# Turning q and k half by transposes, in a new written order, with stage three's first splits moved

## The chip, the core and the metric

The kernel runs on one core of a Trainium2 chip. Its time is device microseconds of one execution; the kernel before took 529.17 us (median of three runs, 526.91 to 531.14). One more execution was profiled: all durations below are from it.

## What is computed

Three blocks follow each other on four sequences of 576 tokens. The first, for 32 heads of 64 columns (four batches, eight heads), adds a coarse attention over four-token means and a local attention within three tokens to each side:

```python
q_d = q.reshape(B, H, S // 4, 4, D).mean(axis=3)      # k_d, v_d alike
out_d = softmax(q_d @ k_d.T / sqrt(D)) @ v_d
mask = abs(pos[:, None] - pos[None, :]) < 4
out_local = softmax(where(mask, q @ k.T / sqrt(D), -1e9)) @ v
x = repeat(out_d, 4, axis=2) + out_local               # B, S, H * D = 512
```

The second block is a gated MLP (`h = gelu(x @ w_in)`, half of it normed and mixed over tokens by `w_sg`, then `w_out`, plus `x`). The third gives every token the two best of four causal attention experts of 64 columns (`x @ wq[e]`, `wk[e]`, `wv[e]`, softmax, `wo[e]`, weighted by the gate's softmax).

## The kernel before, in words

It has three stages, one after the other: `phase1` (local and coarse attention, up to about 134 us of the span), `phase2` (the MLP, to about 340 us) and `phase3` (the experts).

**Stage one** works on 16 units u, one for each pair of heads of a batch. A unit is a chain of short steps, named by one or two letters and the unit's number. `lq`, `lk`, `lv`, `lw` load q, k, v and the v windows (all on SyncE's queue). `Aq` and `Ak` turn q and k on TensorE (`a_pe`, L325), since the products need the 64 columns of a head on partitions: head 0 goes to partitions 0 to 63 of a PSUM tile, head 1 to 64 to 127. `aq` and `ak` copy that to SBUF on ScalarE, `aqd` and `akd` sum groups of four. `Bd` makes the coarse scores, `Bm` the local mask and `Bs` the local scores; `ym yb ey` and `xm xs ex sx` are the two softmaxes, `ne n ny nx` norm them, `Cc` and `Ca` transpose them back (TensorE), `cb` and `ca` copy, `V` sums v in fours on GpSimd, `Du` and `Do` multiply by v, `du` copies, and `dx` adds both into `xT`, the activations, on VectorE (L520). Between the units stand the steps that split `w_in` into two parts (`fetch size clamp bits stt1 stt2 hi lo`), the first split of x (`xhi`, `xlo`) and four blocks of the first product of stage two (`mul`, `gelu`).

TensorE's matmuls come in three tile shapes. Full tiles (128 by 128) serve `Cc`, `Ca`, `mul` and all of stage two. `Aq`, `Ak` and `Du` use two strips of 64 columns that can work side by side, one for each head: a full-height strip on columns 0 to 63 (strip 0) and one on 64 to 127 (strip 1). `Bm`, `Bd`, `Bs` and `Do` use four quarters of 64 by 64. In float32 a product is two records on TensorE, a transpose one.

The string `ORDER` is the order in which all steps are issued, written out by hand: each engine gets its steps in that order. `Steps.run` walks it. It hands each TensorE step one of three `wide` PSUM tiles or two `narrow` ones: the one that a small cost model (the numbers in `do(...)`) thinks is free first, ties going to the first in the list. Of the three wide tiles `pw` was allocated first (named `wide` in traces and orders), then `wide0` and `wide1` (`wide_134` and `wide_135` in the orders below). `GATE` holds a load back until a named TensorE step. So a load can be late for three reasons: its place in the queue, its gate, or the buffer that it fills.

**Stage two** begins with `turn_next`: it transposes the first part of `w_sg` into the first wide PSUM tile of the stage (`pwsg`), which lies on the banks of `pw`. Then follows the first block of `dv`, and so on.

**Stage three** begins with a short run of products for batch 0 (`run(next(first[k], None) for k in "vvpvpvvpp")`: v is one block of 128 tokens for v and the gate, p one block of q or k), and then walks through (batch, expert, block of rows) steps, where `plan` spreads the work that prepares the next batch over the steps of the one before. Each batch's x is split into a high and a low part first (`jobs_split`: ScalarE copies the high part, VectorE subtracts it). The split x of all batches shares one buffer. PSUM is eight banks, handed out in turn; six handed to nothing (`past0` to `past5`) make the first block of v take the seventh. `cmask` and `tmask`, the causal masks, are made by GpSimd at the start.

Of the kernel before, what the change touches and what calls it, by code (L numbers as in the profile page):

```python
# [8 lines left out]
F32 = mybir.dt.float32  # L9
# [4 lines left out]
ALU = mybir.AluOpType  # L14
# [6 lines left out]
def raw(ap):  # L21
# [9 lines left out]
    Du1 yb4 du1 Cc2 lw1 aqd5 Do0 Bm5 fetch2 ne3 akd6 sx4 cb2 Bd5 dx0 ym5 fetch1 ey4 ne4 Bs5 size0 V2 Ca2 Aq6
    ca2 n3 yb5 aq6 ny3 lw2 V3 lw3 ey5 n4 xm5 Aq7 Ak7 clamp0 ak7 Du2 xs5 aq7 aqd6 bits0 nx3 stt10 Do1 stt20 Bm6
    Bd6 du2 dx1 Cc3 ex5 sx5 cb3 Ca3 ny4 ne5 ym6 hi0 ca3 Bs6 aqd7 lk8 yb6 Cc4 akd7 cb4 Do2 xm6 nx4 n5 Bd7 lq8
    xs6 lv4 Bm7 Ca4 nx5 ey6 dx2 ex6 ca4 ym7 Bs7 Du3 lk9 lo0 sx6 lv5 xm7 lq9 Aq8 ny5 ne6 lq10 Ak8 du3 V4 n6 yb7
    size1 xs7 Do3 clamp1 aq8 ey7 lw4 Ca5 nx6 Du4 lk10 ex7 ak8 ca5 V5 aqd8 du4 Cc5 fetch3 bits1 dx3 stt11 size2
    Ca6 akd8 lq11 Ak9 clamp2 bits2 cb5 stt21 Aq9 stt12 ak9 ny6 Do4 sx7 aq9 ca6 Bd8 aqd9 dx4 Bm8 Cc6 ym8 ne7 Bs8
    yb8 stt22 Ak10 Du5 cb6 xm8 ey8 n7 lv7 hi1 Aq10 ak10 xs8 akd9 Bm9 du5 lo1 akd10 size3 Bd9 clamp3 lv6 ny7
    aq10 Bs9 ym9 nx7 ex8 xm9 aqd10 yb9 lw5 fetch4 lk12 Aq11 Cc7 ey9 bits3 lk11 Bd10 lq12 lw6 xs9 Bm10 aq11
    stt13 V6 Do5 aqd11 ym10 lv8 Bs10 cb7 Ca7 yb10 ey10 stt23 ex9 Du6 dx5 sx8 V7 xm10 hi2 Ak12 du6 ca7 sx9 Du7
    lq13 ne8 Ak11 ak12 Aq12 size4 n8 xs10 ny8 ak11 lo2 aq12 clamp4 Bm11 akd12 nx8 Do6 V8 akd11 ne9 du7 aqd12  # L40
    Cc8 n9 Bd11 lk13 Bs11 dx6 lw7 ym11 bits4 fetch5 ex10 lq14 cb8 Ca8 stt14 xm11 yb11 sx10 Aq13 lk14 ey11 nx9
    lw8 Du8 xs11 ca8 aq13 ny9 Ak13 Do7 hi3 aqd13 ne10 stt24 ex11 dx7 n10 sx11 Bm12 Bd12 ak13 du8 Cc9 size5 Ca9
    ym12 ny10 nx10 lv9 akd13 Bs12 cb9 clamp5 Cc10 xm12 ca9 ne11 Ak14 n11 cb10 yb12 ak14 lo3 bits5 xs12 Aq14 Do8
    Bm13 hi4 ey12 lk15 lq15 ny11 V9 stt15 Bd13 aq14 ex12 dx8 Bs13 Ak15 aqd14 lv10 ym13 Aq15 stt25 nx11 ak15
    yb13 sx12 aq15 akd15 akd14 Du9 lw9 ne12 V10 Ca10 du9 xm13 Cc11 n12 xhi0 Bd14 ca10 xs13 nx12 lv11 xhi2 xlo2
    Do9 dx9 cb11 ym14 ey13 xhi1 Bm14 Ca11 ny12 Bs14 ca11 Du10 xm14 xs14 lw10 lv12 yb14 aqd15 Cc12 V11 hi5 Ca12
    du10 lw11 xhi3 fetch7 Bd15 V12 lo5 cb12 ey14 Bm15 xlo3 xlo1 Do10 xlo0 Bs15 Du11 ex13 lv13 ca12 sx13 ne13
    dx10 ym15 du11 lo4 ex14 size7 yb15 lw12 xm15 mul1 xs15 ey15 mul2 clamp7 ex15 fetch6 gelu1 sx14 Du12 bits7
    ne14 n13 gelu2 stt17 n14 V13 small ny13 du12 Do11 Do12 sx15 lw13 stt27 nx14 hi7 ne15 nx13 mul0 ny14 n15
    dx12 Cc13 dx11 size6 gelu0 Cc14 cb13 Ca14 clamp6 lo7 Ca13 Du13 ca14 cb14 lv14 ny15 ca13 lw15 lv15 lw14 Cc15  # L50
# [89 lines left out]
def tile_pooled_local_attention_gmlp_moe_attention(  # L140
# [103 lines left out]
    def phase1():  # L244
        with tc.tile_pool(name="s1", bufs=2, reuse_waits="tile") as p:
# [42 lines left out]
            def whole(u, nm):  # L288
                return WHOLE[nm](u)
# [224 lines left out]
            def d_x(u):  # L514
# [14 lines left out]
                "wide": [pw] + [px["p"].tile([P, 2, 512], F32, name=f"wide{i}", bufs=1) for i in range(2)],  # L529
# [3 lines left out]
            def unit(u):  # L533
# [449 lines left out]
    def phase3():  # L983
        with tc.tile_pool(name="m2", bufs=2, reuse_waits="tile") as p:
            cmask = p.tile([P, S + 64], F32, name="cmask", bufs=1)
            pool.memset(cmask, 0.0)
            pool.affine_select(out=cmask[:, S - 64 :], in_=cmask[:, S - 64 :], pattern=[[-1, P]],
                               compare_op=ALU.is_ge, fill=NEG, base=0, channel_multiplier=1)
# [16 lines left out]
            tmask = p.tile([P, HS], F32, name="tmask", bufs=1)  # L1005
            pool.memset(tmask, 0.0)
            for h in range(2):
                pool.affine_select(out=tmask[64 * h : 64 * h + 64, HS - 64 :], in_=tmask[64 * h : 64 * h + 64, HS - 64 :],
                                   pattern=[[-1, 64]], compare_op=ALU.is_ge, fill=NEG, base=0, channel_multiplier=1)
# [299 lines left out]
            def jobs_split(b):  # L1309
# [4 lines left out]
                x = xs[b] = cx["p"].tile([P, 2, KT, S], F32R, tag="xhl", name=f"xhlb{b}")  # L1314
# [138 lines left out]
```

## Time and profile before

| | us |
|---|---|
| median of three runs | 529.17 |
| the profiled execution | 527.32 |
| its span, first to last instruction | 525.6 |
| stage one, to its last product on TensorE | 133.5 |
| stage two | to 339.8 |
| stage three | to 525.6 |

[...] The timeline gives merged instructions of one engine: start, length, engine, line, operation, tiles, shapes, how many, and in brackets how long the engine had idled before it and what ended that. PE is TensorE's matmuls, PEld its weight loads, DVE VectorE, ACT ScalarE, POOL GpSimd, SP SyncE with a q for its queue. Matmul records overlap, so their lengths don't add up: the distance from start to start is what a step takes.

### The profile page before, as it was taken

What the parts mean: (1) busy time and instruction counts of PE and PEld (TensorE: products, weight loads), DVE (VectorE), ACT (ScalarE), POOL (GpSimd) and SP (SyncE); (2) the same over time, 40 slices, a digit from 0 to 9 for tenths busy, and PEclk for the clock granted to TensorE, in tenths of its full rate; (3) what the DMA queues carried; (4) which work ended last, traced back from release to release, by engine and by line L of the source; (5) the groups of instructions that cost most, each with busy time, mean ns of one, the idle gap of its engine ahead of it and who ended that gap; (6) DMA issues with size and microseconds to landing.
All of it is one profiled execution on the core that took longest, in us unless ns stands there. A gap on an engine that the chain in (4) does not pass through costs nothing.

```text
span 525.6 us, 13672 instructions
## 1 busy us (share of the span) xinstructions
PE 507.8 (97%) x5405; PEld 463.3 (88%) x5405; DVE 351.0 (67%) x913; ACT 268.0 (51%) x676; POOL 254.7 (48%) x390
## 2 busy tenths in 40 slices
PE   9998999899899999999999999998999999999996
PEld 6887888789689899989998999998988989998885
DVE  4786999895769864642344147348799678868862
ACT  2875787784363450134013403337668558655762
POOL 4777989899153630360035106745437334333540
PEclk9998999999899999999999999999999999999999
DMA  7999799576400220000000001200000100011013
GB/s 197 200 198 196 188 213 215 122 191 151 139 20 1 82 60 1 1 0 1 1 1 0 1 1 30 72 2 1 1 2 1 42 21 21 22 42 42 16 65 101
DMA packets 43415, 35.02 MB, mean 67 GB/s; under 512 B 29976, under 2 KB 36376, under 8 KB 43352
## 3 DMA queue, kind: packets, MB, share of 16 engines
q1 hardware_dynamic: 43352, 34.15, 27.3%
q8 instruction: 43, 0.70, 0.6%
q14 instruction: 20, 0.16, 0.1%
HBM read 29.42 MB, written 4.72 MB: 65 GB/s over the span
## 4 chain that ended last, share of the span: by engine, by line
PE 62%; DVE 7%; issue 2%; ACT 1%; POOL 1%; ACTq 0%; DVEq 0%; POOLq 0%
PE f L74 10%; PE e L74 9%; PE du L74 7%; PE dv L74 5%; PE v L74 5%; PE i L74 5%; PE sc L74 5%; PE av L74 4%; PE gq L74 4%; PE gk L74 4%; PE tr L74 4%; DVE kl L1048 1%; DVE z L880 1%; DVE xhlb L239 1%; POOL vn L239 0%
## 5 line engine op out<-in xcount | busy, mean ns | idle before, releaser
L239 POOL TENSOR_TENSOR gT<-z,gT 128x576 fp32r<-128x576 f32 x15 | 23.0, 1537 | 105.3 <-ACT gT L211 105.3
L74 PE MATMUL e<-wsgT,vn 128*128 128x288 f32 x384 | 56.4, 296 | 0.0
L74 PEld LDWEIGHTS e<-wsgT,vn 128*128 128x128 f32 x384 | 53.0, 188 | 0.1
L74 PE MATMUL f<-gT,wouts 128*128 128x288 f32 x384 | 51.8, 295 | 0.0
L74 PEld LDWEIGHTS f<-gT,wouts 128*128 128x128 f32 x384 | 51.4, 188 | 0.0
L211 ACT CAST gT<-z 128x576 fp32r<-128x576 f32 x16 | 10.8, 674 | 78.1 <-DVE z L883 78.1
L74 PE MATMUL dv<-win,xhla 128*128 128x512 f32 x192 | 47.7, 405 | 0.1
L908 DVE TENSOR_TENSOR xT<-f,xT 128x576 f32<-128x576 f32 x16 | 12.1, 758 | 50.5 <-PE f L74 50.5
L74 PEld LDWEIGHTS dv<-win,xhla 128*128 128x128 f32 x192 | 36.7, 194 | 8.5 <-ACT vg L793 0.5
L74 PEld LDWEIGHTS du<-xhla,win 128*128 128x128 f32 x288 | 38.5, 188 | 0.3
L74 PE MATMUL du<-xhla,win 128*128 128x288 f32 x288 | 38.7, 295 | 0.0
L1190 POOL TENSOR_SCALAR xT<-xT,sden,wt 128x128 f32<-128x128 f32 (+3 forms) x32 | 20.7, 645 | 35.8 <-DVE sden L1188 31.5
L1190 POOL TENSOR_SCALAR Xs<-Xs,sden,wt 128x128 f32<-128x128 f32 (+3 forms) x32 | 19.6, 613 | 25.6 <-DVE sden L1188 14.9
L74 PE MATMUL gq<-xhlb,w 128*128 128x288 f32 x192 | 29.6, 301 | 0.1
L520 DVE TENSOR_TENSOR xT<-wide,up 64x288 f32<-64x288 f32 (+1 forms) x48 | 21.7, 452 | 11.7 <-PE wide L74 10.5
L74 PE MATMUL gk<-xhlb,w 128*128 128x288 f32 x192 | 29.1, 300 | 0.0
L74 PEld LDWEIGHTS gq<-xhlb,w 128*128 128x128 f32 x192 | 26.2, 189 | 0.6 <-DVE xhlb L239 0.4
L74 PE MATMUL i<-w,yT 128*128 128x512 f32 (+1 forms) x102 | 26.5, 395 | 0.0
L1176 DVE CUSTOM_DVE_ANT_0 xT<-sc,cmask 128x128 f32<-128x128 f32 (+4 forms) x40 | 19.3, 484 | 10.6 <-PE sc L74 10.1
L74 PEld LDWEIGHTS gk<-xhlb,w 128*128 128x128 f32 x192 | 26.2, 188 | 0.2
L798 DVE BATCH_NORM_STATS2 bst<-vg 128x6 f32<-128x512 f32 x18 | 12.5, 693 | 20.5 <-ACT vg L793 20.5
L1183 ACT ACTIVATE xT<-xT,smx 128x128 f32<-128x128 f32 (+4 forms) x40 | 24.3, 607 | 3.2 <-DVE smx L1176 2.7
(206 smaller groups left out, 1359.0 us busy)
## 6 DMA issues: line engine op xcount, KB each, us to landing
vw<-in_v_dram SPq DMA_DIRECT2D x31, 160.0 KB
k<-in_k_dram SPq DMA_DIRECT2D x16, 288.0 KB
q<-in_q_dram SPq DMA_DIRECT2D x16, 288.0 KB
v<-in_v_dram SPq DMA_DIRECT2D x16, 256.0 KB
wst<-in_moe_w_in_dram SPq DMA_DIRECT2D x8, 512.0 KB
out_dram<-os SPq DMA_DIRECT2D x15, 256.0 KB
wst<-in_moe_w_out_dram SPq DMA_DIRECT2D x4, 512.0 KB
wsg<-in_moe_w_sg_dram SPq DMA_DIRECT2D x4, 288.0 KB
```

The source lines that it names most:

```text
L74: self.last = fn(*args, **kw)
L211: act.copy(o, i)
L239: e_lo.tensor_tensor(lo, src, raw(hi), op=ALU.subtract)
L520: dve.tensor_tensor(xT[dst, b, hp, a * HS : (a + 1) * HS].rearrange("c (s j) -> c s j", j=4), d["po"][src, a, :HS].rearrange("c (s j) -> c ...
L798: dve.bn_stats(stt, g)
L880: dve.scalar_tensor_tensor(y2, o[:, :, :HS], gcol[:, dt : dt + 1], bbc.rearrange("p (a s) -> p a s", a=2), op0=ALU.mult, op1=ALU.add)
L908: dve.tensor_tensor(dst, os_[mt][:, :, :HS], dst, op=ALU.add)
L1048: dve.tensor_tensor(dst, o[R_[h], :HS], raw(T[h][R_[h], c]), op=ALU.subtract)
L1176: dve.tensor_tensor_reduce(out=X[:, c0:c1], in0=os_[i][:, : c1 - c0], in1=tmask if i else cmask[:, z + c0 : z + c1] if r < NQ else cmask[: ...
L1183: act.activation(X, X, AF.Exp, bias=mx, scale=-1.0, accum_out=den)
L1190: pool.tensor_scalar(X, X, den, w, op0=ALU.mult, op1=ALU.mult)
```

## The change

In `a_pe`, head 0 is now turned by six transposes, and then head 1 by six products; before, each of the six columns groups was two products, one for each head. The planner's cost of the step goes from 1.02 to 0.84. `ORDER` and `GATE` are written anew. The list of wide tiles is `wide0`, `pw`, `wide1`.

In stage three the split of batch 1 moves into the opening run, between its products; it has a buffer of its own, so that `xT` of batch 1 is free from then on, and `Xs[1]` and the masks live there. The masks are made after the opening run, and one bank instead of six is passed over.

```diff
-    lk0 Ak0 lq0 lq1 lk1 Aq0 ak0 lq2 lk2 Aq1 aq0 Ak1 Bm0 aqd0 akd0 ak1 Bd0 aq1 Bs0 Aq2 aqd1 aq2 lq3 aqd2 Ak2
...
-    bits6 nx15 stt16 mul3 cb15 V14 stt26 du13 Ca15 Do13 ca15 dx13 V15 Du14 gelu3 hi6 Du15 du15 lo6 Do14 Do15
-    du14 dx14 dx15
+    lq0 Aq0 aq0 lk0 Ak0 aqd0 lq1 ak0 lk1 Aq1 Ak1 lq2 ak1 lk2 lv1 akd0 Bm0 Bd0 aq1 ym0 aqd1 Bs0 V1 akd1 Ak2 ak2
...
+    lw15 Ca14 cb15 ca14 dx12 Cc14 V15 lo6 Ca15 Do13 cb14 Do14 Du14 ca15 dx13 hi7 du14 Du15 lo7 small Do15 dx14
+    du15 dx15
...
             def a_pe(u, nm):
                 d = st[u]
                 t = d["p" + nm] = wide(f"t{nm}{u}")
-                for j in range(6):
-                    o = t[:, j // 3, (j % 3) * R6 : (j % 3 + 1) * R6]
-                    if whole(u, nm):
-                        for h in range(2):
-                            pe.matmul(o[64 * h : 64 * h + 64], d[nm][:, h, j], ident[:R6, :R6], start=True, stop=True)
...
+                def part(j):
+                    return t[:, j // 3, (j % 3) * R6 : (j % 3 + 1) * R6]
+
+                if whole(u, nm):
+                    for j in range(6):
+                        pe.transpose(part(j)[:64], d[nm][:, 0, j], ident[:R6, :R6])
+                    for j in range(6):
+                        pe.matmul(part(j)[64:], d[nm][:, 1, j], ident[:R6, :R6], start=True, stop=True)
...
-                "wide": [pw] + [px["p"].tile([P, 2, 512], F32, name=f"wide{i}", bufs=1) for i in range(2)],
+                "wide": [px["p"].tile([P, 2, 512], F32, name="wide0", bufs=1), pw,
+                         px["p"].tile([P, 2, 512], F32, name="wide1", bufs=1)],
...
-                do("Aq", {"PE": 1.02 if whole(u, "q") else 0.58}, a_pe, "lq0", args=("q",), ring="wide",
+                do("Aq", {"PE": 0.84 if whole(u, "q") else 0.58}, a_pe, "lq0", args=("q",), ring="wide",
...
-            Xs = [old[:, :NX], p.tile([P, NX], F32, name="Xs", bufs=1)]
+            old1 = xT[:, 1].rearrange("p k s -> p (k s)")
+            Xs = [old[:, :NX], old1[:, :NX]]
+            cmask, tmask = old1[:, NX : NX + S + 64], old1[:, NX + S + 64 : NX + S + 64 + HS]
...
-                x = xs[b] = cx["p"].tile([P, 2, KT, S], F32R, tag="xhl", name=f"xhlb{b}")
+                if b == 1:
+                    x = xs[b] = Halves(p.tile([P, 2, 2, S], F32R, tag="yT", name="xhi")
+                                       .rearrange("p a h s -> p (a h) s"),
+                                       p.tile([P, KT, S], F32R, name="xlo", bufs=1))
+                else:
+                    x = xs[b] = cx["p"].tile([P, 2, KT, S], F32R, tag="xhl", name=f"xhlb{b}")
...
-            for i in range(6):
-                bank(f"past{i}")
+            dve.memset(bank("past")[:, :1], 0.0)
...
-            first = {"v": jobs_v(0), "p": jobs_proj(0, 0, ("q0", "k0", "q1", "k1"))}
-            run(next(first[k], None) for k in "vvpvpvvpp")
+            first = {"v": jobs_v(0), "p": jobs_proj(0, 0, ("q0", "k0", "q1", "k1")), "x": jobs_split(1)}
+            run(next(first[k], None) for k in "vvxpxvpxvxvpp")
+            set_masks()
...
-                    plan(k0, SPL, jobs_split(b + 1), 4)
+                    if b:
+                        plan(k0, SPL, jobs_split(b + 1), 4)
```

The order tells what moves at the end of stage one. TensorE before, from the last transposes (`ident,X` is `Ca15`, rows with `aTs` are `Do`, with `bTs` are `Du`, units by their buffers) to the first `pwsg`; the middle rows of each `Do` are left out by a line of dots:

```order
L74 MATMUL wide_134<-ident,X_2187 128x128 x5
L74 MATMUL wide<-aTs_90,vw_84 64x60 x2
...
L74 MATMUL narrow_136<-bTs_91,vd_88 64x144 x4
L74 MATMUL narrow_137<-bTs_92,vd_86 64x144 x4
L74 MATMUL wide_134<-aTs_89,vw_85 64x60 x2
...
L74 MATMUL wide<-aTs_90,vw_83 64x60 x2
...
L74 MATMUL pwsg_2559<-ident,wsg_2541 128x128 x4
```

And now:

```order
L84 MATMUL wide_134<-ident,X_2206 128x128 x5
L84 MATMUL wide<-aTs_90,vw_84 64x60 x2
...
L84 MATMUL wide_135<-aTs_89,vw_85 64x60 x2
...
L84 MATMUL narrow_136<-bTs_91,vd_88 64x144 x4
L84 MATMUL narrow_137<-bTs_92,vd_86 64x144 x4
L84 MATMUL wide_134<-aTs_90,vw_83 64x60 x2
...
L84 MATMUL pwsg_2559<-ident,wsg_2541 128x128 x4
```

The last step, `Do15`, filled `wide` (the banks of `pwsg`) before and fills `wide_134` now; the last user of `wide` is now `Do13`.

VectorE at the opening of stage three, from the last sum of stage two (`f_3`) on, before (`lg` are gate logits, `qs` and `kl` low parts of q and k):

```order
L908 TENSOR_TENSOR xT<-f_3_4459,xT 128x576
L1004 MEMSET xT 128x64
L1084 COPY lg_4543<-v_4_4546 64x4 x2
L1084 COPY lg_4544<-v_4_4546 64x4 x2
L1080 COPY lg_4543<-v_0_4559 128x4
L1048 TENSOR_TENSOR qs_0_0_4591<-gq_0_0_4578,qs_0_0_4591 64x288
L1048 TENSOR_TENSOR qs_0_1_4592<-gq_0_0_4578,qs_0_1_4592 64x288
L1080 COPY lg_4543<-v_1_4595 128x4
L1048 TENSOR_TENSOR kl_4519<-gk_0_0_4612,ks_0_0_4625 64x288
```

And now:

```order
L923 TENSOR_TENSOR xT<-f_3_4459,xT 128x576
L1017 MEMSET xT 128x64
L1384 MEMSET past 128x1
L1103 COPY lg_4525<-v_4_4528 64x4 x2
L1103 COPY lg_4526<-v_4_4528 64x4 x2
L249 TENSOR_TENSOR xlo<-xT,xhi 128x576
L1099 COPY lg_4525<-v_0_4541 128x4
L249 TENSOR_TENSOR xlo<-xT,xhi 128x576
L1067 TENSOR_TENSOR qs_0_0_4579<-gq_0_0_4566,qs_0_0_4579 64x288
L1067 TENSOR_TENSOR qs_0_1_4580<-gq_0_0_4566,qs_0_1_4580 64x288
L1099 COPY lg_4525<-v_1_4587 128x4
L249 TENSOR_TENSOR xlo<-xT,xhi 128x576
```

The four `xlo` (the fourth follows after two rows of `kl`) stood, as `xhlb`, some 50 rows further down, in two pairs between the first softmaxes of experts 0 and 1.

## Rows read from the trace of the kernel before

**Rows 1.** The page, its first part: busy us, share, instructions.
```profile
PE 507.8 (97%) x5405; PEld 463.3 (88%) x5405; DVE 351.0 (67%) x913; ACT 268.0 (51%) x676; POOL 254.7 (48%) x390
```

**Rows 2.** Windows: us; busy PE, PEld, DVE, ACT, POOL; clock; DMA share; GB/s.
```profile
50.00:60.00 10.00, 9.86 (x243) 8.61 (x237) 9.79 (x18) 9.10 (x26) 9.62 (x12) 1.00 0.75 183
...
130.00:140.00 10.00, 7.53 (x153) 6.21 (x152) 7.01 (x20) 2.72 (x7) 2.00 (x3) 0.83 0.38 101
...
180.00:340.00 160.00, 159.78 (x1120) 154.96 (x1118) 71.52 (x118) 45.74 (x77) 51.21 (x54) 1.00 0.06 14
340.00:350.00 10.00, 9.37 (x75) 9.37 (x76) 3.19 (x12) 3.17 (x9) 6.44 (x21) 1.00 0.01 2
```

**Rows 3.** Groups by form, TensorE, 0 to 144 us: shapes, count, busy, mean ns.
```profile
L74 PE MATMUL wide<-ident,k 96*64 96x96 f32 x384 | 19.7, 253 | 0.0
...
L74 PE MATMUL wide<-ident,X 128*128 128x128 f32 x80 | 11.9, 282 | 0.2 <-POOL Y L454 0.2
```

**Rows 4.** Timeline of TensorE: transposes of full height, then two steps A and the next.
```profile
28.98 0.82 PE L74 MATMUL wide<-ident,Y 128*72 128x128 f32 x6
29.73 0.33 PE L74 MATMUL wide<-mb,identb 64*64 64x320 bf16 x4
...
37.87 2.20 PE L74 MATMUL wide<-ident,q 96*64 96x96 f32 x48
...
39.91 1.16 PE L74 MATMUL wide<-ident,k 96*64 96x96 f32 x24
```

**Rows 5.** Timeline of TensorE where `Bd` ends and `Bs` begins.
```profile
15.94 0.27 PE L74 MATMUL wide<-kT,qT 64*64 64x64 f32 x1
15.94 0.28 PE L74 MATMUL narrow<-kd,qd 64*64 64x144 f32 x1
...
16.05 0.29 PE L74 MATMUL narrow<-kd,qd 64*64 64x144 f32 x2
```

**Rows 6.** Timeline where stage one ends and stage two begins.
```profile
130.33 6.69 SPq L87 DMA_DIRECT2D wsg<-in_moe_w_sg_dram  x3
...
132.06 1.39 PE L74 MATMUL wide<-aTs,vw 64*64 64x60 f32 x80
...
133.00 2.82 DVE L520 TENSOR_TENSOR xT<-wide,up 128x288 f32<-128x288 f32 x6 [0.47 <-ACT up L512]
...
135.93 0.74 PE L74 MATMUL pwsg<-ident,wsg 128*128 128x128 f32 x5 [2.47 <-issue]
...
136.42 4.60 PE L74 MATMUL dv<-win,xhla 128*128 128x512 f32 x12
...
141.32 3.05 PE L74 MATMUL dv<-win,xhla 128*128 128x512 f32 x12
```

**Rows 7.** Timeline where stage two ends and stage three begins.
```profile
339.82 0.76 DVE L908 TENSOR_TENSOR xT<-f,xT 128x576 f32<-128x576 f32 x1 [2.43 <-PE f L74]
...
340.63 1.71 PE L74 MATMUL v<-w,xremb 128*128 128x260 f32 x12 [0.85 <-DVE xT L908]
```

**Rows 8.** Timeline around the split of batch 1 in stage three.
```profile
364.50 1.43 DVE L239 TENSOR_TENSOR xhlb<-xT,xhlb 128x576 fp32r<-128x576 f32 x2
...
366.18 1.23 ACT L211 CAST xhlb<-xT 128x576 fp32r<-128x576 f32 x2
...
366.80 0.63 PE L74 MATMUL tr<-ident,xT 128*128 128x128 f32 x4 [1.37 <-DVE smx L1176]
...
367.72 1.51 DVE L239 TENSOR_TENSOR xhlb<-xT,xhlb 128x576 fp32r<-128x576 f32 x2
...
368.61 0.43 PEld L74 LDWEIGHTS gq<-xhlb,w 128*128 128x128 f32 x3 [0.37 <-DVE xhlb L239]
```

**Rows 9.** Timeline: the mask on GpSimd, and VectorE's first use of it.
```profile
339.85 0.63 POOL L986 MEMSET cmask<- 128x640 f32 x1 [1.09 <-PE f L74]
...
357.77 0.29 DVE L1176 CUSTOM_DVE_ANT_0 xT<-sc,cmask 128x128 f32<-128x128 f32 x1
```

**Rows 10.** Timeline of TensorE, the longest gap inside stage one.
```profile
44.03 0.46 PE L74 MATMUL wide<-aTs,vw 64*64 64x57 f32 x16 [1.84 <-issue]
```

More of the change, by code (lines that the diff above doesn't have):

```diff
@@ L31 @@
[L31 to L50, printed above, removed]
@@ new lines @@
+    Ak14 V10 ak14 stt15 ne12 Ak15 lw10 xhi0 akd14 Du9 du9 Cc11 Bm14 ak15 cb11 stt25 Bd14 akd15 Do9 xhi1 n12
+    lv12 ym14 Bs14 xhi3 xhi2 dx9 lw11 Du10 yb14 Ca11 ex13 fetch6 du10 aqd15 ny12 V11 ca11 xlo3 Cc12 Bd15 xm14
+    Do10 xs14 nx12 ey14 xlo1 V12 lv13 cb12 Bm15 dx10 Du11 hi4 ex14 Ca12 xlo0 lo4 xlo2 hi5 Bs15 Do11 ym15 du11
+    ca12 sx13 ne13 Du12 xm15 mul1 yb15 fetch7 dx11 ey15 mul2 n13 du12 size7 xs15 sx14 ex15 size6 sx15 lv14
+    clamp7 ne15 clamp6 ne14 V13 bits6 ny13 gelu1 stt16 stt26 bits7 gelu2 n15 nx13 lw13 stt17 V14 mul3 gelu3
@@ L56, with __init__, __getitem__ @@
+    lw12 lo5 Ca13 ca13 Cc13 mul0 cb13 lw14 Do12 nx15 n14 hi6 lv15 gelu0 ny15 Du13 Cc15 du13 stt27 ny14 nx14
+    lw15 Ca14 cb15 ca14 dx12 Cc14 V15 lo6 Ca15 Do13 cb14 Do14 Du14 ca15 dx13 hi7 du14 Du15 lo7 small Do15 dx14
+    du15 dx15
+""".split()
+class Halves:
+    def __init__(self, hi, lo):
+        self.parts = hi, lo
+    def __getitem__(self, k):
+        return self.parts[k[1]][k[:1] + k[2:]]
 GATE = dict(x.split(":") for x in """
-    lv0:Bd0 lw0:Bm3 lw3:Aq6 lv4:Bd6 lw4:Ak8 lk5:Ak2 lv5:Cc4 lw5:Bs8 lq6:Bd3 lq7:Bs3 lv7:Do4 lq8:Bd6 lw8:Ca8
@@ L61 @@
+    fetch0:Ca0 fetch2:Bm8 fetch3:Do5 fetch4:Bs9 fetch5:Bd11 fetch6:Do9 fetch7:Du11
 """.split())
@@ L327, in a_pe @@
                 t = d["p" + nm] = wide(f"t{nm}{u}")
-                for j in range(6):
-                    o = t[:, j // 3, (j % 3) * R6 : (j % 3 + 1) * R6]
-                    if whole(u, nm):
-                        for h in range(2):
-                            pe.matmul(o[64 * h : 64 * h + 64], d[nm][:, h, j], ident[:R6, :R6], start=True, stop=True)
-                    else:
-                        pe.transpose(o, d[nm][:, j].rearrange("r h d -> r (h d)"), ident[:R6, :R6])
+                def part(j):
[6 more added lines that the diff above has]
+                else:
+                    for j in range(6):
+                        pe.transpose(part(j), d[nm][:, j].rearrange("r h d -> r (h d)"), ident[:R6, :R6])
             def turn(u, nm, eng):
@@ L984, in phase3 @@
         with tc.tile_pool(name="m2", bufs=2, reuse_waits="tile") as p:
[L985 to L988, printed above, removed]
             tri = p.tile([P, E, E], F32, name="tri", bufs=1)
@@ L1001, in phase3, with set_masks @@
             old = xT[:, 0].rearrange("p k s -> p (k s)")
-            Xs = [old[:, :NX], p.tile([P, NX], F32, name="Xs", bufs=1)]
+            old1 = xT[:, 1].rearrange("p k s -> p (k s)")
+            Xs = [old[:, :NX], old1[:, :NX]]
+            cmask, tmask = old1[:, NX : NX + S + 64], old1[:, NX + S + 64 : NX + S + 64 + HS]
             Xt = old[:, NX : NX + S + 64]
             dve.memset(Xt[:, S:], 0.0)
[L1005 to L1009, printed above, removed]
+            def set_masks():
+                pool.memset(cmask, 0.0)
+                pool.affine_select(out=cmask[:, S - 64 :], in_=cmask[:, S - 64 :], pattern=[[-1, P]],
+                                   compare_op=ALU.is_ge, fill=NEG, base=0, channel_multiplier=1)
+                pool.memset(tmask, 0.0)
+                for h in range(2):
+                    r = slice(64 * h, 64 * h + 64)
+                    pool.affine_select(out=tmask[r, HS - 64 :], in_=tmask[r, HS - 64 :], pattern=[[-1, 64]],
+                                       compare_op=ALU.is_ge, fill=NEG, base=0, channel_multiplier=1)
             qts = [p.tile([P, 2, 2, 64], F32R, name=f"qt{i}", bufs=1) for i in range(2)]
```

31 lines of the change are left out of this document (23 added, 8 removed).

## The prediction

> **What bounds the kernel now.** First the page's busy times: TensorE is busy 507.8 us, 97% of the span [rows 1], and no other engine passes 67%. So I look for the places where TensorE stands idle, works at half clock, or does work that goes away. The windows tell the stages apart [rows 2]. In the middle of stage one (50 to 60) TensorE is busy 9.86 of 10 us, but VectorE 9.79 and GpSimd 9.62 too: a shorter TensorE step there is worth its length only as long as the other two keep up. From 130 to 140, where stage one turns into stage two, TensorE is busy 7.53, at a granted clock of 0.83. From 180 to 340 it is busy 159.78 of 160: stage two has nothing to give, and the change does not touch it. From 340 to 350, the opening of stage three, VectorE is busy 3.19 and ScalarE 3.17: room for more.
>
> **Part 1: the step A.** Before, twelve products of a step were 24 records (384 over 16 steps `Ak`), while the five transposes of a `Ca` are five records (80 over 16) [rows 3]. Two steps A, 48 records, take from 37.87 to 39.91, 2.04 us [rows 4]: 1.02 a step, 85 ns for each of 12 pairs, of which one record runs on strip 0 and one on strip 1, side by side. What does one such record take alone? Six full-height transposes of 128 columns take 28.98 to 29.73, 0.75 with the change of tile shape behind them [rows 4]. 85 ns for 96 columns is 113 ns for 128; six are 0.68, which leaves 0.07 for the change of shape. So a lone record of 96 columns takes about the 85 ns of a pair, and one strip does not run faster when the other is empty.
>
> Now strip 0 has 6 records (0.51 us) and strip 1 has 12 (1.02 us). Strip 1 sets the step's length, and it has as many records as before. **Removing a quarter of the records thus removes nothing from the step**; it only leaves strip 0 idle for half of it. The planner's 0.84 is a number that orders steps, not a measurement.
>
> There is a loss: the transposes now stand ahead of the products, so strip 1 starts late unless records may pass one another. They may a little: a `Bs` record starts at 15.94, ahead of three `Bd` records that stand before it in the order (one at 15.94, two at 16.05) [rows 5]. With three passed, the first product waits for the starts of at most two of the remaining transposes, 2 x 0.085 = 0.17; with all passed, for none. I take the middle, 0.085, once for each run of steps A that stand next to each other on TensorE (17 in the new order for 32 steps, and inside a run the next step's transposes fill the idle strip): 17 x 0.085 = **+1.4**. The ends are 0 and 17 x 5 x 0.085 = 7.2, none or all five starts awaited.
>
> [...]
>
> **Part 2: the written order.** The end of stage one is where I can price it. The last `Do` products end about 133.4; VectorE's six sums `dx` run 133.00 to 135.82 on the results; `pwsg` starts at 135.93, after 2.47 us of idle [rows 6]. It cannot start earlier, because it lies on the banks of `wide`, which the last step `Do15` filled and the last `dx` read. In the change `Do15` fills `wide_134`, and the last user of `wide` is `Do13`, whose `dx13` stands ahead of `Do15`. `pwsg` waits for nothing then but its data: the load of `wsg` was issued at 130.33, its three parts took 6.69 together, and the first was in by 135.93 [rows 6]; I take it to be in by the new end as well. If it is not, that wait comes back (the last rival). Left is a change of tile shape and issue, which I put at 0.3: **-2.2** (ends 0 and -2.47). The cost behind the gap goes with it: the first block of `dv` takes 4.60 us, the second, of the same shape, 3.05 [rows 6], since the granted clock falls after the pause (0.83 over these 10 us). 4.60 - 3.05 = 1.55, **-1.6** (ends 0 and -1.6). What is late next is `dv` itself: its input x was split long before, and only the last units' sums come after it.
>
> Inside stage one the changed `ORDER` and `GATE` move everything. I counted the changes of tile shape in TensorE's two orders: 71 before, 67 now; 4 x 0.07 = **-0.3**. The longest gap, 1.84 us before 44.03, has no releaser but issue [rows 10], nothing in that place that the order would mend; I keep it in kind at another place, at 0, and for all gaps and half clocks of the new order together I take ends of twice that gap, -3.5 and +3.5. The DMAs are the same transfers on the same queue; a load that comes late in the new order is inside these ends.
>
> **Part 3: stage three.** The first `v` waited 0.85 us for VectorE's last `xT` sum of stage two [rows 7], because its bank, the seventh, was the one that the sum read. Now it takes a bank that was free long before: **-0.85**, ends 0 and -0.85 (v needs only x of batch 0, which was ready). In its place a one-element memset of the passed bank stands behind that sum on VectorE; nothing on TensorE's path waits for it.
>
> The split of batch 1 stood at 364.50 to 369.23: two pairs of VectorE subtractions, 1.43 and 1.51, and ScalarE copies [rows 8]. TensorE waited 1.37 before `tr` at 366.80, for a softmax step queued on VectorE next to the split, and its weight loads 0.37 at 368.61 for the split itself [rows 8]: 1.74 together. I count both as gone, **-1.74**, ends 0 and -1.74. The 2.94 us of VectorE work now lie in the opening, where 3.19 of 10 us are busy [rows 2], and four ScalarE copies of 0.62 beside 3.17. That cover holds: 3.19 + 2.94 = 6.1 of 10. If it did not hold, the reading of the logits and of q and k for the first scores would be late, by no more than one subtraction, 0.72.
>
> The masks: GpSimd's first memset takes 0.63 and stood at 339.85; the first reader on VectorE is at 357.77 [rows 9]. The other pieces (a smaller memset, three selects) I put at twice that, 1.9 in all. Now they follow GpSimd's copies of the opening. 6.44 of the first 10 us are busy there [rows 2], so GpSimd should be through them well before 357.77 - 1.9 = 355.9: 0, and as an end +1.9, if the copies fill all the time up to the reader.
>
> **Sum.** 527.3 (the profiled execution, in the table above, 1.85 under the median) - 2.2 - 1.6 - 0.3 - 0.85 - 1.74 + 1.4 = **522.0**. The median of 529.17 is the looser figure: the three runs spread over 4.2 us, so I do not add the 1.85 and keep it in the range. With the ends of the terms combined loosely, this case alone runs 518 to 526.
>
> **Rivals, with their chances.**
> - *My forecast*, strip 1 as floor, the end of stage one and the opening shortened: 0.47.
> - *The step does get shorter.* If a lone record is quicker than one of a pair, the step scales with its records: 18 of 24, 0.77 for 1.02, -0.255 x 32 = -8.2, with the +1.4 gone: 522.0 - 1.4 - 8.2 = about 512.5, and as VectorE and GpSimd are nearly as full [rows 2], a third of it lost: **515**. For it: nothing but the count of records [rows 3]. Against it: the 0.75 of the full-height transposes [rows 4]. 0.15.
> - *Strict order in the step.* Records start only in program order: then a product starts with the last transpose, 5 x 0.085 late, and the next step's first transpose not before the last product starts. From start to start that is 5 x 0.085 + 11 x 0.085 = 1.36, +0.34 x 32 = +10.9 for the +1.4: 522.0 - 1.4 + 10.9 = **532**. Rows 5 speak against it, by one record only. 0.12.
> - *Slower: transposes and products do not share the array.* If a strip that transposes shuts out the other, the step is 6 x 0.085 + 12 x 0.085 = 1.53, +0.51 x 32 = +16.3, and with a change of shape of 0.07 on either side +0.65 x 32 = +20.8: 522.0 - 1.4 + 16.3 to 20.8 = **537 to 541**. It decides from the point where a step takes 1.02 + (534.5 - 520.6) / 32 = 1.45. No row of before shows a transpose on one strip beside a product on the other, so nothing excludes it. 0.12. [...]
> - *The new order opens waits of its own.* A late load, or a second pause that costs the clock as the one before `dv` did, gives back 2.47 + 1.55 and one gap of the size of rows 10's: 522.0 + 4.0 + 1 to 2 = **527**. 0.14.
>
> **Range and chances.** 0.47 and 0.15 reach from 514 to 526, the 527 case and the strict order to 535; left out is nearly all of the slower rival and the low edge, under 0.2: 514 to 535. A measurement of this kernel tells about 1% from no change, 5.3 us: under 523.9 is faster, over 534.5 slower. Faster: the case of 515, and about three quarters of my own case (its 518 to 526 is cut at 523.9): 0.15 + 0.35 = 0.50. Slower: the rival of that name, and a little of the strict order: 0.14. Within 1%: the rest, 0.36.
>
> **What would show it.** The distance from start to start of two adjacent steps A: 1.02 if I am right, 0.77, 1.36 or 1.5 and more by the rivals; and whether the first product record lies among the transposes or behind them. The gap before `pwsg`: 0.3, and the first `dv` block as long as the second. The first `v` right behind the last `f` product, no subtraction between 360 and 369 and no gap before `tr` there, masks made before the first score's maximum. I am wrong if A's distance changes by a tenth or more, or if stage one's inner gaps, which I put at nothing, move by several us.

## The result: slower by 1.4%, where 1.4% faster was forecast

The changed kernel takes 533.50 us (median of seven runs, 532.57 to 533.94), the kernel before 527.09 (seven runs, 520.94 to 531.14): a ratio of 1.0141, 95% interval 1.0093 to 1.0188. The ratio leaves out executions more than 1.5% above the fastest of their kernel, here two of the kernel before (529.17 and 531.14); the two medians alone give 1.012. The forecast was 522.0, a gain of 1.4% on the 529.17 that then stood for the kernel before. The profiled execution took 533.05, of it 531.3 the span; 525.6 was the span before. Where the 5.7 us come from, by the times at which `pwsg` and the first `v` start:

| us | before | after | difference | forecast |
|---|---|---|---|---|
| stage one, to the first `pwsg` | 135.9 | 146.5 | +10.5 | -1.1 |
| of it steps A | 35.2 | 54.3 | +19.1 | +1.4 |
| of it all other steps and waits | 99.4 | 90.9 | -8.6 | -2.5 |
| stage two, `pwsg` to the first `v` | 204.7 | 202.1 | -2.6 | -2.45 |
| stage three | 185.0 | 182.7 | -2.25 | -1.74 |

(A step's time is the sum of the distances from each of its records to the next record on TensorE, whatever that is; the 1.25 us before the first record are left out of the two middle rows.)

**Step A.** The page of the changed kernel, part 1, which answers to [rows 1]:

```profile
PE 521.7 (98%) x5213; PEld 474.2 (89%) x5213; DVE 350.5 (66%) x914; ACT 269.0 (51%) x676; POOL 252.7 (48%) x390
```

TensorE's busy time rose by 13.9 us, with 192 records fewer. The groups by form, which answer to [rows 3]:

```profile
L84 PE MATMUL wide<-ident,k 96*64 96x96 f32 x288 | 29.0, 250 | 0.0
...
L84 PE MATMUL wide<-ident,X 128*128 128x128 f32 x80 | 11.9, 279 | 0.0
```

The records fell from 384 to 288, a quarter, as counted. Their busy time rose from 19.7 to 29.0. Fewer records are busy for longer in sum, so they no longer run beside one another. The timeline of TensorE after shows it in two adjacent steps:

```profile
23.83 1.82 PE L84 MATMUL wide<-ident,k 96*64 96x96 f32 x18
25.58 1.82 PE L84 MATMUL wide<-ident,q 96*64 96x96 f32 x18
27.33 0.70 PE L84 MATMUL narrow<-kd,qd 64*64 64x144 f32 x7
```

25.58 - 23.83 = 1.75 us from start to start, against 1.02 before [rows 4]. Single records of the first step start 0.0825 apart: six transposes from 23.83, then, 0.176 after the last of them (24.27 to 24.45), twelve product records, and 0.177 after the last product (25.41 to 25.58) the next step's transposes. No product starts among the transposes. 18 x 0.0825 = 1.49; the two passages between the kinds add 0.094 each, and the second record after each passage comes 0.03 to 0.05 late. If a transpose did share the array with a product, and a record passed three others as in [rows 5], the step would be 3 x 0.0825 + 9 x 0.0825 = 0.99 long, by these distances.

**What a transpose of 64 columns is.** In another place `Ca`, full tiles, stands right ahead of a step A. After:

```profile
91.81 0.77 PE L84 MATMUL wide<-ident,X 128*128 128x128 f32 x5
92.41 1.79 PE L84 MATMUL wide<-ident,k 96*64 96x96 f32 x18
```

And before, ahead of the step A of [rows 4] that starts at 37.87:

```profile
37.18 0.76 PE L74 MATMUL wide<-ident,X 128*128 128x128 f32 x5
```

After, the step A follows 0.60 us behind the start of the five full-tile transposes; record by record its first transpose comes 0.109 behind the last of them, which is the distance inside `Ca` itself. Before it was 0.69, and 0.203 behind the last. So by these distances the transposes of 64 columns go as full tiles do: 0.109 from a full tile to them, with no change of shape in it, and 0.176 from them to a strip. That the shape is paid for, and not the change from transposes to products, other places of the changed kernel show: products on full tiles start 0.028 behind the last full-tile transpose (`tr` to `gq`), products on strips or quarters 0.202 behind it (`tr` to `av`, `X` to `Bs`). The row's form, 96*64, does not tell this.

**The waits of stage one.** The windows that answer to [rows 2]:

```profile
50.00:60.00 10.00, 10.00 (x246) 8.68 (x246) 7.57 (x15) 5.94 (x16) 9.25 (x14) 1.00 0.89 204
...
140.00:150.00 10.00, 7.32 (x161) 6.19 (x160) 7.07 (x20) 3.28 (x8) 2.63 (x3) 1.00 0.65 187
```

TensorE is busy 10 of 10 in the middle of stage one, VectorE 7.57 where it was 9.79. The waits of TensorE between 2 and 132 us, before:

```profile
PE wide L74 <- issue: 4.9, 6, 1.8
PE narrow L74 <- issue: 1.2, 2, 0.9
```

And after, all that is left of them:

```profile
PE narrow L84 <- POOL vd L388: 0.4, 1, 0.4
PE wide L84 <- DVE X L424: 0.2, 1, 0.2
PE narrow L84 <- DVE wmn L699: 0.2, 1, 0.2
```

6.1 us of waits named issue are gone, and with them the half clock that followed the longest one [rows 10]. The windows of before show it (the granted clock, as a share of full speed, is the third number from the end):

```profile
44.00:46.00 2.00, 1.97 (x32) 1.63 (x32) 1.39 (x4) 0.00 (x0) 1.92 (x5) 0.60 0.89 166
46.00:48.00 2.00, 2.00 (x12) 1.80 (x11) 1.97 (x3) 0.39 (x1) 1.44 (x2) 0.55 0.42 95
```

From 44.5 to 47.5 each window of 0.5 us shows 0.50. These 4 us at 0.60 and 0.55 cost up to 1.7 us. Together that is most of the 8.6 that the other steps give back.

**The end of stage one.** The timeline that answers to [rows 6]:

```profile
137.42 2.88 SPq L97 DMA_DIRECT2D vw<-in_v_dram  x3
...
140.82 0.50 SPq L97 DMA_DIRECT2D bbc<-in_moe_b_sg_dram  x1
141.48 6.07 SPq L97 DMA_DIRECT2D wsg<-in_moe_w_sg_dram  x4
...
146.45 0.73 PE L84 MATMUL pwsg<-ident,wsg 128*128 128x128 f32 x5 [2.68 <-DVE xrema L225]
146.95 3.05 PE L84 MATMUL dv<-win,xhla 128*128 128x512 f32 x12
```

The pause ahead of `pwsg` is still there, 2.68 for 2.47. `pwsg` waits for VectorE, for PSUM and for a load, and the row names the one that came last by the profile. It was the load: SyncE's queue, which had waited 3.53 us on the semaphore of the first part of `wsg`, went on at 146.34, and TensorE's wait on the same semaphore ended at 146.35. The load of `wsg` stands behind the window load of unit 15 (in the queue at 137.42, when `Do12` had freed its buffer) and behind the 288 KB of `bbc`; before, its first part was issued at 126.60. The clock stayed at 1.00 this time (140 to 150, above), and the first `dv` block takes 3.05, where it took 4.60.

**Stage three.** The timeline that answers to [rows 7, 8, 9]:

```profile
348.58 1.60 PE L84 MATMUL v<-w,xremb 128*128 128x260 f32 x12
348.78 0.76 DVE L923 TENSOR_TENSOR xT<-f,xT 128x576 f32<-128x576 f32 x1 [2.44 <-PE f L84]
...
351.82 0.76 DVE L249 TENSOR_TENSOR xlo<-xT,xhi 128x576 fp32r<-128x576 f32 x1
...
363.90 0.63 POOL L1020 MEMSET xT<- 128x640 f32 x1
...
373.32 0.42 PEld L84 LDWEIGHTS tr<-ident,xT 128*128 128x128 f32 x4 [0.29 <-POOL xT L1209]
```

`v` waits for nothing; the subtractions stand in the opening (351.82 is the first). The last row answers to this one of before:

```profile
366.76 0.42 PEld L74 LDWEIGHTS tr<-ident,xT 128*128 128x128 f32 x4 [1.57 <-POOL xT L1190]
```

The weight loads of this `tr` waited 1.57 us and wait 0.29; its products waited 1.37 [rows 8], and now follow the product before them within 0.1. The masks are made at 363.90, and the first maximum on VectorE starts at 365.61, 17.0 us behind the first `v`; it was 17.1 before.

### The profile page after: what moved, and what is told of

It reads as the page before. It is cut to its first block, busy times and chain, and to the rows that moved or that the text cites. A ratio compares the mean times of both kernels' runs of the same rounds, so it can differ in the third digit from the quotient of the medians.

```text
span 531.3 us, 13296 instructions
## 1 busy us (share of the span) xinstructions
PE 521.7 (98%) x5213; PEld 474.2 (89%) x5213; DVE 350.5 (66%) x914; ACT 269.0 (51%) x676; POOL 252.7 (48%) x390
## 4 chain that ended last, share of the span: by engine, by line
PE 61%; DVE 5%; ACT 2%; issue 1%; POOL 1%; DVEq 0%; POOLq 0%
PE f L84 10%; PE e L84 8%; PE du L84 7%; PE dv L84 5%; PE v L84 5%; PE i L84 5%; PE sc L84 5%; PE av L84 4%; PE gq L84 4%; PE gk L84 4%; PE tr L84 4%; DVE z L895 1%; DVE xT L1195 1%; POOL vn L249 0%; DVE wmn L699 0%
## 5 line engine op out<-in xcount | busy, mean ns | idle before, releaser
L1209 POOL TENSOR_SCALAR xT<-xT,sden,wt 128x128 f32<-128x128 f32 (+1 forms) x64 | 39.0, 609 | 57.9 <-DVE sden L1207 43.8
L1202 ACT ACTIVATE xT<-xT,smx 128x128 f32<-128x128 f32 (+4 forms) x72 | 42.3, 587 | 9.8 <-DVE smx L1195 7.6
L1195 DVE CUSTOM_DVE_ANT_0 xT<-sc,xT 128x128 f32<-128x128 f32 (+4 forms) x72 | 35.0, 487 | 18.3 <-PE sc L84 17.4
L84 PE MATMUL dv<-win,xhla 128*128 128x512 f32 x192 | 46.2, 395 | 0.1
L84 PE MATMUL tr<-ident,xT 128*128 128x128 f32 x192 | 33.0, 274 | 0.5 <-DVE smx L1195 0.5
L534 DVE TENSOR_TENSOR xT<-wide,up 64x288 f32<-64x288 f32 (+1 forms) x48 | 21.8, 454 | 11.8 <-PE wide L84 11.2
L84 PE MATMUL wide<-ident,q 96*64 96x96 f32 x288 | 29.1, 250 | 0.0
L84 PE MATMUL wide<-ident,k 96*64 96x96 f32 x288 | 29.0, 250 | 0.0
L84 PEld LDWEIGHTS wide<-ident,q 96*64 96x64 f32 x288 | 23.9, 128 | 4.3 <-issue 0.4
L84 PEld LDWEIGHTS tr<-ident,xT 128*128 128x128 f32 x192 | 23.8, 140 | 4.3 <-issue 0.9
L84 PEld LDWEIGHTS wide<-ident,k 96*64 96x64 f32 x288 | 23.9, 128 | 4.1 <-issue 0.4
```

The costliest lines, as they stand in the source:

```text
L84: self.last = fn(*args, **kw)
L534: dve.tensor_tensor(xT[dst, b, hp, a * HS : (a + 1) * HS].rearrange("c (s j) -> c s j", j=4), d["po"][src, a, :HS].rearrange("c (s j) -> c ...
L1195: dve.tensor_tensor_reduce(out=X[:, c0:c1], in0=os_[i][:, : c1 - c0], in1=tmask if i else cmask[:, z + c0 : z + c1] if r < NQ else cmask[: ...
L1202: act.activation(X, X, AF.Exp, bias=mx, scale=-1.0, accum_out=den)
L1209: pool.tensor_scalar(X, X, den, w, op0=ALU.mult, op1=ALU.mult)
```

## The experiments

Each ratio is to the kernel before as it ran beside the experiment. Its median was 525.2 us beside the first four, 526.5 beside the next four, 526.3 beside the last three, and 527.1 above; so a difference of medians from different groups is good to some 2 us.

**Products in pairs again.** The changed kernel, with the step A of before:

```diff
-                    for j in range(6):
-                        pe.transpose(part(j)[:64], d[nm][:, 0, j], ident[:R6, :R6])
                     for j in range(6):
-                        pe.matmul(part(j)[64:], d[nm][:, 1, j], ident[:R6, :R6], start=True, stop=True)
+                        for h in range(2):
+                            pe.matmul(part(j)[64 * h : 64 * h + 64], d[nm][:, h, j], ident[:R6, :R6], start=True, stop=True)
```

> The changed kernel, but step A as before: for each column group a product for head 0 and one for head 1, 24 records side by side on two strips. Everything else (written order, wide tiles, stage three) as changed. Theory (transposes and products do not share the array; A went from 1.02 to 1.70 us start to start): A is back at 1.02 to 1.10 and, if the new order keeps TensorE fed, stage one loses 0.6 to 0.7 x 32 = 19 to 22 us: 512 to 515 us. Rival 1 (VectorE and GpSimd hold stage one, and the new order had few stalls only because TensorE was slower): A is back but 8 us of stalls come with it, 521 to 524. Rival 2 (the new order itself is the cost): 531 to 534.

Measured 521.7 us, 0.9938 of before (0.9901 to 0.9975). The time is that of the first rival. A is back at 35.1 us in all, 19.2 less, and the other steps and waits of stage one take 96.7 for 90.9: 5.8 of it are lost again. The waits of TensorE, 2 to 132 us, and one of them on the timeline:

```profile
PE wide L84 <- issue: 6.4, 8, 2.2
...
52.37 0.41 PE L84 MATMUL wide<-kT,qT 64*64 64x64 f32 x11
54.97 0.68 PE L84 MATMUL wide<-kT,qT 64*64 64x64 f32 x29 [2.19 <-issue]
```

A step `Bs` stops after 11 of its 40 records, and goes on 2.2 us later, with nothing released in between. VectorE's or GpSimd's pace, as that rival put it, is not what the row shows; what it is, the kernel with twice the instructions tells.

**The new step alone.** The kernel before, with nothing but the new loops in `a_pe`.

> The kernel before with the new step A alone (six transposes, then six products); order, tiles and stage three as before. Theory: A takes 1.70, +0.6 x 32 = +19 us if the 15 us of stalls in the old order stay (546), less by what A fills of them, at most 8 (538). Rival (the new order is the cost, A is not): 526 to 529. The forecast's own step (A longer by the lead alone): +1.4, 528.5.

536.58 us, 1.0238 (1.0182 to 1.0294). A takes 54.2, +19.0, and 8.0 are given back: the waits named issue fall from 6.1 to 0.4. In the old order as in the new one the step itself costs 11 to 12 us (536.6 - 525.2 = 11.4 and 533.5 - 521.7 = 11.8, medians).

**Stage three alone.** The kernel before, with the diff's edits from `phase3` on.

> The kernel before with the edits of stage three alone (split of batch 1 in the opening, masks later, one bank passed over). The forecast's terms: 0.85 + 1.74 = -2.6 us, so 524.5 against 527.1. Rival: the waits move (tr or the first softmaxes late instead), within 0.5 us of before.

522.89, 0.9955 (0.9913 to 0.9996). The median fell by 2.3. In the profile the time from `v` to the end is 182.7 for 185.0, to 0.1 that of the changed kernel. The edits of stage three are a gain, near the size forecast.

**Heads in turn, both by products.**

```diff
-                    for j in range(6):
-                        pe.transpose(part(j)[:64], d[nm][:, 0, j], ident[:R6, :R6])
-                    for j in range(6):
-                        pe.matmul(part(j)[64:], d[nm][:, 1, j], ident[:R6, :R6], start=True, stop=True)
+                    for h in range(2):
+                        for j in range(6):
+                            pe.matmul(part(j)[64 * h : 64 * h + 64], d[nm][:, h, j], ident[:R6, :R6], start=True, stop=True)
```

> The changed kernel with step A in the changed order, head 0 first and head 1 second, but both heads by products: 12 records on strip 0, then 12 on strip 1. It tells the order from the operation. If records pass one another freely, A takes 1.02 from start to start and the time is that of the products in pairs. If they may pass only a few (or none), the strips run one behind the other: up to 23 x 0.0825 = 1.9 to 2.0 us, some 9 us over the changed kernel, 540 to 543. Side by side within a step at all, when two steps follow each other: the next step's strip 0 beside this one's strip 1. If the operation alone forbids the sharing, A is 1.02 to 1.1 here.

528.61, one run. The timeline of TensorE:

```profile
22.32 1.67 PE L84 MATMUL wide<-ident,k 96*64 96x96 f32 x21
23.76 0.30 PE L84 MATMUL wide<-ident,q 96*64 96x96 f32 x1
23.84 0.25 PE L84 MATMUL wide<-ident,k 96*64 96x96 f32 x1
...
24.06 1.62 PE L84 MATMUL wide<-ident,q 96*64 96x96 f32 x21
```

Records of `q` start while `k` still has three to go (at 23.84, 23.92 and 24.00). Inside the step, too, strip 1's first record starts with the ninth of strip 0's twelve: three are passed, as in [rows 5], no more. 23.76 - 22.32 = 1.44 from start to start; I had the long end of 1.9 to 2.0, and 540 to 543 for the time, since I did not count the overlap with the next step. Two strips do share the array in this order, so it is the operation, not the order, that takes the sharing away from the changed step. The order has a price of its own where both heads are products: steps A take 50.9 us in all, against 35.1 in pairs, since no more than three records are passed.

**`small` moved ahead.** The changed kernel, in `ORDER` alone:

```diff
-    lw15 Ca14 cb15 ca14 dx12 Cc14 V15 lo6 Ca15 Do13 cb14 Do14 Du14 ca15 dx13 hi7 du14 Du15 lo7 small Do15 dx14
+    small lw15 Ca14 cb15 ca14 dx12 Cc14 V15 lo6 Ca15 Do13 cb14 Do14 Du14 ca15 dx13 hi7 du14 Du15 lo7 Do15 dx14
```

> The changed kernel with one step of the written order moved: the two constants' loads (`small`) go ahead of the window load of unit 15 in SyncE's queue, not behind it. Theory (the 2.7 us before pwsg are the late load of wsg, issued at 141.48 behind the window load and the 288 KB of `small`, arriving at 146.34): wsg is issued 1.0 us earlier and has the queue for itself, the gap shrinks by 1.5 to 2.5 us, 531 to 532. Rival (pwsg waits for VectorE's sums as before): the gap and the time stay, 533.5.

530.84, 1.0102 (1.0064 to 1.0139) of before, 2.7 under the changed kernel by medians and 2.2 by the profiled spans. `wsg` is issued at 139.16, and the pause is gone:

```profile
139.16 5.35 SPq L97 DMA_DIRECT2D wsg<-in_moe_w_sg_dram  x4
141.13 4.28 DVE L534 TENSOR_TENSOR xT<-wide,up 128x288 f32<-128x288 f32 x9 [2.52 <-PE wide L84]
143.38 0.50 PEld L84 LDWEIGHTS pwsg<-ident,wsg 128*128 128x128 f32 x5
```

`pwsg` starts at 143.38, while VectorE still sums (to 145.41): the new list of wide tiles does free it from the last `dx`, and the late load alone had held it.

**Both.** Products in pairs and `small` ahead.

> Products in pairs in the new order (521.7), with `small` moved ahead as well: a candidate for the fastest. If the late load holds pwsg there too: 1.0 to 1.6 less, 520 to 521. If something else holds it (a pause of 1.6 before pwsg in that kernel): 521.7.

518.25 us (four runs, 517.79 to 519.34), 0.9845 (0.9791 to 0.9899): the fastest of all kernels here, 1.5% under the one before. By medians it gains 3.4 on the pairs alone, more than the 1.6 us of their pause; between the two profiled spans it gains 1.4 (516.5 for 517.9). The runs of the pairs spread from 517.7 to 527.8, and nothing here shows a second cause.

**Transposes and products alternating.**

```diff
                     for j in range(6):
                         pe.transpose(part(j)[:64], d[nm][:, 0, j], ident[:R6, :R6])
-                    for j in range(6):
                         pe.matmul(part(j)[64:], d[nm][:, 1, j], ident[:R6, :R6], start=True, stop=True)
```

> The changed kernel with transposes and products alternating: one transpose, one product (two records), six times. Theory (each passage between a transpose and a product drains the array and costs some 0.095 us): 18 x 0.0825 + 12 x 0.095 = 2.6 us a step, +0.9 x 32 = +29, at most 8 of it hidden: 555 to 563. Rival (they do not share the array, but only the first passage into a step costs): 1.5 to 1.7 us, 530 to 534. If they shared it when adjacent: 1.02, under 525.

612.59, one run, above every expectation. At full clock one transpose and one product (two records) take 0.512 from start to start (25.309 to 25.821): 3 x 0.0825 and two passages of 0.13 each, over the 0.095 expected. That a passage drains the array was the theory's guess: the run shows its length alone. At that rate 32 steps take 98 us (32 x 6 x 0.512), which is 44 of the 79 us that this kernel takes more than the changed one. The rest, 35, I put down to the clock: over the whole run 0.925 of it was granted (0.999 in the changed kernel), which is some 45 us of full clock less in 610.9, enough for it. A window of stage one:

```profile
10.00:50.00 40.00, 40.00 (x310) 25.18 (x309) 11.85 (x17) 10.35 (x32) 8.44 (x15) 0.64 0.26 69
```

TensorE counts as busy for 40.00 of 40 us and is granted 0.64 of its clock; if the lower level is the 0.50 of 44.5 to 47.5 in the kernel before, that is an estimate of 29 us at it (40 x 0.36 / 0.50). It runs 310 records where the changed kernel runs 675, at 1.00. The same records in two groups kept the full clock, so the low clock came with the alternation too; how, no run shows.

**Fewer data loads.** Products in pairs, with the window loads of units 3 to 15 left out, whose local sums then use old windows:

```diff
                 vw = st.setdefault(u, {})["vw"] = vws[u % 3]
+                if u >= 3:
+                    return
```

> Products in pairs in the new order, with the window loads (packets of 256 bytes) of units 3 to 15 left out, so that those units use old windows: the load on the DMA engines falls by a fifth or more. It asks what ends TensorE's waits named issue (6.4 us, eight of them, in the middle of a step). Theory A (instructions arrive late because the data loads crowd the queues): the waits fall under 2 us and the time to 515 to 518. Theory B (TensorE simply reads its instructions faster than they come, whatever the data load): 5 to 7 us of waits stay, 519 to 522.

518.53. The load on the DMA engines between 50 and 90 us falls from 0.87 to 0.57; the waits named issue are 4.9 us, at four places, the longest 2.5. That is under theory B's 5 to 7 by a little and far over theory A's 2. The time is 3.2 us under that of the pairs with all loads (0.5 between the profiled spans) and lies between the two theories. It is that of the kernel with `small` ahead, and a like reason is at hand: `wsg` is not held up behind a window load, and `pwsg` follows the last products without a pause (132.02). So theory B stands for the waits.

**Twice the instructions.** Products in pairs, each cut in two:

```diff
-                            pe.matmul(part(j)[64 * h : 64 * h + 64], d[nm][:, h, j], ident[:R6, :R6], start=True, stop=True)
+                            for c in range(2):
+                                pe.matmul(part(j)[64 * h : 64 * h + 64, 48 * c : 48 * c + 48], d[nm][:, h, j],
+                                          ident[:R6, 48 * c : 48 * c + 48], start=True, stop=True)
```

> Products in pairs in the new order, each product cut into two of 48 columns: the same columns through the array, twice the instructions in step A. It asks again about the waits named issue. Theory (TensorE runs out of instructions: it reads them faster than they come): these waits grow well over the 6.4 us of products in pairs, to 12 us or more, and the time to 528 or more. Rival (they come from something else, as a data load): waits stay at 5 to 8 us, A itself grows by the shorter records' overhead alone, 522 to 526.

538.45, one run. The waits, 2 to 132 us:

```profile
PE wide L84 <- issue: 11.7, 13, 2.5
PE narrow L84 <- POOL win L228: 0.2, 1, 0.2
```

Steps A take 53.6 us here, as long as in the changed kernel (54.3) and a little longer than with the heads in turn (50.9). Those two, with half the records of this one or fewer, have no wait named issue; this one has 11.7 us of them, just under the 12 expected. (The time is no sign for either side, since steps A alone grew by 18.5.) So the waits follow the number of instructions in a given time, as the theory that TensorE runs out of them had it.

The traces show where. Counted from 0 along TensorE's own instructions (matmuls, weight loads, semaphore steps), all 68 waits named issue that are longer than 0.15 us, between 2 and 132 us and over all kernels here, leave 193 or 194 when their number is divided by 256; the 48 waits with another releaser leave remainders all over. The pages list a DMA queue of the kind instruction (q8) that moved 43 packets of 16 KB for the pairs and 49 for this kernel: six more for 768 more records, so one packet for 128 records with their weight loads, which are 256 instructions (768 / 6 = 128). Each of the 68 waits ends 1.2 to 1.8 us after one of these packets has landed; the one at 54.97 in the pairs, 1.54 after 53.43. I read this as TensorE having used up the 256 instructions of a packet, and standing until the next packet is there; the counts and the landings are measured, the link between them is not shown by itself. Beyond the pace at which instructions are used up, and the data loads of the experiment before this one, I varied nothing that could make a packet late.

**Full tiles for the later units.** Two candidates built on the fastest kernel: q and k (or q alone) of units 9 to 15 loaded with both heads side by side and turned by six full-height transposes, by a number in the kernel:

```diff
-    WHOLE = {"q": lambda u: u < 16, "k": lambda u: u < 16}
+    WHOLE = {"q": lambda u: u < 9, "k": lambda u: u < 9}
```

> The fastest so far (pairs, `small` early, 518.25), with q and k of units 9 to 15 loaded with the two heads' columns side by side (the path that the kernel has for it) and turned by six full-height transposes for both heads: 0.58 for 1.02 a step, 14 steps, a quarter of the records. If TensorE and its instructions bound the second half of stage one: up to 14 x 0.44 = 6.2 less, 512 to 515. If the loads, which then have 256-byte packets, come late: 520 or more.

> The same for q alone, units 9 to 15: 7 x 0.44 = 3.1 less at most, 515 to 517; over 519 if the loads come late.

521.63, 0.9914 (0.9876 to 0.9952), and 520.26, 0.9877 (0.9809 to 0.9946): no better than 518.25. For both tensors, 3.5 us of new waits are for ScalarE's copies of k:

```profile
PE wide L84 <- issue: 5.5, 4, 2.4
PE wide L84 <- ACT kT L221: 3.5, 3, 1.7
```

The order was not written for steps of that length, and I did not write another. Where nothing holds it, such a step takes 0.55 to 0.65, as expected, but the profiled execution also ran 13.7 us of stage one at the lower clock (0.50 over 28 to 32, 64 to 66 and 88 to 90), after pauses of 1.8, 1.7 and 2.4 us; the fastest kernel's had none there. Over all runs the mean granted clock was 0.989, against 0.998. For q alone it was 0.997, and 2.0 us of new waits are for loads (k, the windows and q), as expected if they came late.

## Why the prediction was wrong

- **Step A, the failed step.** "Strip 1 sets the step's length" took it that a transpose on strip 0 runs beside a product on strip 1, as two products do. No row of before showed that pair, and I gave the sharing to the operation because the strips had it. The runs show transposes that go as full tiles do, 0.109 behind one, with no product of the other strip among them and 0.176 from the one kind to the other: +19.1 us in all, 0.60 a step ((54.3 - 35.2) / 32), in place of +1.4 in all. That was my slower rival, at 0.12, and its price too: +0.51 to +0.65 a step. That rival deserved more than the 0.12 that the absence of a row left it.
- **The lead.** Three records are passed, as I read it, but in the runs only by products on another strip or quarter; inside the changed step none was passed. Strict order, the second rival's, does not hold between strips: with the heads in turn, `q` records start at 23.76 and 23.89 ahead of `k` records at 23.84 and 23.92.
- **The inner gaps, put at 0 with ends of 3.5.** They fell by about 6 us, and 5.8 to 8.0 come or go with the length of A in either order. The prediction saw in [rows 10] a wait with no releaser but issue, and kept it for that reason. The kernel with twice the instructions shows what such a wait hangs on (11.7 us of them for 6.4): as I read it, a longer step with fewer instructions leaves time for the next ones to come, so a slower A is partly paid back. That is why the time is 533.5 and not the rival's 537 to 541. It lies in the stated range of 514 to 535, and near the 532 of strict order, by luck: the range was made of other cases, and this pay-back was in none.
- **The pause before `pwsg`, -2.2.** The wait on the last `dx` went, and the load of `wsg` took its place; the prediction named that as the last rival's way. It had also misread [rows 6]: the 6.69 us are those of three issues in SyncE's queue with the waits between them, and the first part had been issued at 126.60. Moving one load took 2.7 us off.
- **The first `dv` block, -1.6.** It came by luck: the pause stayed (2.68), and the clock did not fall (1.00; the block took 3.05).
- **Changes of tile shape, -0.3.** My count of 67 held the new steps for one shape. Each has a passage inside, and the 21 that follow a strip (another A, or `Du`) have one ahead as well, and a passage cost 0.094, not 0.07.
- **Stage three.** `v`, -0.85: right. The split, -1.74: right in kind, with -2.25 measured for the stage. The masks: right.

## What to carry to other kernels

That two products run beside each other (1.02 us a step here) does not tell that a transpose and a product do (1.75): before counting on it, look for a row with that very pair, and where there is none, price the case without sharing as the likely one. A gain or loss on the fullest engine is worth its length less the waits that it fills or uncovers: here 19 us of longer steps cost 11 to 12. A wait of TensorE with no releaser can be a wait for its own instructions, as I read the 68 here: look whether such waits stand 256 instructions, or a multiple of that, apart, as these did. A load behind another load's buffer wait is late by that wait (here SyncE's queue stood 7.1 us, up to 137.42, for the buffer of the window load, with `wsg` behind it), so a change in the order of steps is read in the DMA queue as well.

## What the chip did that I had not expected

- A pause of about 2.5 us did not always bring half clock: 2.47 us before `pwsg` were followed by it in the kernel before (0.83 over 130 to 140, 0.50 over 137 to 139), 2.68 in the changed one, and 2.47 with the new step alone, were not. A pause of 1.84 was followed by it too (0.60 over 44 to 46), one of 2.19 in the pairs was not (1.00).
- 40 us in which TensorE never counts as idle ran at 0.64 of its clock, with the alternating step.
- The number of its instructions can hold TensorE, as I read it (all 68 waits named issue at 193 or 194 by 256): 24 records a step in 1.1 us (35.1 / 32) gave 6.4 us of waits over stage one, 24 in 1.6 us none (50.9 / 32), 48 in 1.7 us 11.7 (53.6 / 32).
- A float32 transpose of 64 columns went as a full tile does: 0.109 behind a full-tile transpose, 0.176 ahead of a product on a strip, and nothing on the other strip beside it.
